# Zero stores sized by (batch, kv-heads), with four extra calls of 1.6 MB each: before the first softmax, after the output product of the last two groups and in the last group's K scores

## Chip, cores and metric

One Trainium2 chip, one core. The metric is device time of one execution in microseconds (us), lower is better. Runs are compared with runs of the kernel before on the same chip.

## The reference, cut to what matters

Decode attention over a window of the last W = 1024 of Sk = 4096 positions, in parallel with a GELU-gated MLP, forward and backward. Only the last 1024 positions of the K and V caches take part, so the gradients of the first 3072 are zero and have to be written:

```python
B, Sq, D = 4, 1, 512
Hq, Hkv, Sk, Dh = 32, 8, 4096, 128
W = min(4096, max(256, Sk // 4))                 # 1024
k = jnp.repeat(k_cache[:, :, Sk - W:, :], rep, axis=1)
v = jnp.repeat(v_cache[:, :, Sk - W:, :], rep, axis=1)
...
return x + _A_ref(xn, ...) + _B_ref(xn, ...)     # and jax.vjp of all of it
```

The gradients of K and V (out_2, out_3) are bfloat16 of 4 x 8 x 4096 x 128 each; their zero parts are 2 x 4 x 8 x 3072 x 128 x 2 B = 50.3 MB.

## The kernel before

The attention runs in NT = 4 groups t of two kv-heads. Loads go out on the sync engine, computed gradients on GpSimd, zeros on the scalar engine. Names in the profile: kb and vb are loads of K and V, osb_o and osb_q are staging tiles with gradients of the output and query weights, dx_b is the gradient of the input and the last thing computed, ztile holds the zeros. odq(t, 0) is the output product of group t with V (the recorded texts call the place after it the first "next-group product"), odq(t, 1) the dQ product. A zero store is placed behind the last scalar copy (`last`) that the program has at this point. The program text is no schedule: the build may move instructions of the compute engines within their engine.

```python
K0 = Sk - W                                   # 3072
outp = ctx.enter_context(tc.tile_pool(name="outp", bufs=3))   # staging of weight gradients (osb_o, osb_q, ...)
...
ZP = P // 2
ZW = K0 // ZP * Dh                            # 64 partitions of 12,288 B for one (batch, head)
...
ZG = 4
zlist = [(og, b, g) for b in range(B) for g in range(0, G, ZG) for og in (out_2, out_3)]   # 16 stores of 3.1 MB

def zeros(n):
    zs = ztile[0:P:P // ZP, :]
    zsrc = bass.AP(tensor=zs.tensor, offset=zs.offset, ap=[list(zs.ap[0]), [0, ZG], [1, ZW]])
    for _ in range(min(n, len(zlist))):
        og, b, g = zlist.pop(0)
        z = store(nc.scalar, og[b, g:g + ZG, 0:K0, :].rearrange("g (m j) d -> m g (j d)", m=ZP), zsrc, "zeros",
                  ["rest", "zeros"])
        tc.add_manual_dep(z.ins, last[-1].ins.name, ...)
...
def scores(t, k):                             # k = 0: K scores, k = 1: V (dP)
    for g in range(GP):
        for b in range(B):
            ...                               # transposes, copy, matmuls
            tick(2)                           # two pieces of deferred gradient work
            if b == 1 and (g, k) != (0, 0):
                zeros(1)
...
for t in range(NT):
    masks(t)
    scores(t, 0); softmax(t);   dvdk(t, 0)
    scores(t, 1); softmax_d(t); dvdk(t, 1)
    odq(t, 0)
    if t + 1 < NT: pre(t + 1)
    odq(t, 1); fin(t)
    load_next(t)                              # K, V of group t+1 (second head), K, V and weights of t+2
    dw(t)
tick(len(bg))
zeros(len(zlist))                             # whatever is left: 3 stores
```

Of the kernel before, what the change touches and what calls it, by code (L numbers as in the profile page):

```python
# [18 lines left out]
def kernel(  # L19
# [24 lines left out]
    nc = tc.nc  # L44

    B, Sq, D = A_x.shape
    _, G, Sk, Dh = A_k_cache.shape
# [4 lines left out]
    K0 = Sk - W  # L52
# [4 lines left out]
    GP = 2  # L57
    NT = G // GP
# [25 lines left out]
    def evac(out, in_, n, half=False, eng=None):  # L84

        eng = "dve" if half else eng
        ca, cd = (190 + n) / 1.2, (120 + (n / 2 if half else n)) / 0.96
        if eng is None:
            eng = "act" if load["act"] + ca <= load["dve"] + cd else "dve"
        load[eng] += ca if eng == "act" else cd  # L90
        if eng == "act":
            last.append(nc.scalar.copy(out=out, in_=in_))  # L92
            return last[-1]
        return nc.vector.tensor_copy(out=out, in_=in_)  # L94

    def store(eng, out, in_, kind, apart):

        d = eng.dma_start(out=out, in_=in_)  # L98
        for k in apart:
            tc.declare_no_dep(d.ins, group=k, reason="stores write disjoint parts of the outputs")  # L100
        tc.add_to_no_dep_group(kind, d.ins)
        return d
# [9 lines left out]
    for eng, dst, src in ((nc.sync, dy_b, grad_out), (nc.scalar, x_b, A_x)):  # L112
        eng.dma_start(out=dst[:], in_=bass.AP(tensor=src.tensor, offset=src.offset,
                                                  ap=[[D, B], [0, RB], [1, D]]))
# [42 lines left out]
    ZP = P // 2  # L157
    ZW = K0 // ZP * Dh
# [82 lines left out]
    def load_next(t):  # L241

        if t + 1 < NT:
            load_kv(t + 1, 0, 1)
            load_kv(t + 1, 1, 1)
        if t + 2 < NT:
            load_w(t + 2)
            load_kv(t + 2, 0, 0)
            load_kv(t + 2, 1, 0)


    ZG = 4
    zlist = [(og, b, g) for b in range(B) for g in range(0, G, ZG) for og in (out_2, out_3)]

    def zeros(n):

        zs = ztile[0:P:P // ZP, :]
        zsrc = bass.AP(tensor=zs.tensor, offset=zs.offset, ap=[list(zs.ap[0]), [0, ZG], [1, ZW]])
        for _ in range(min(n, len(zlist))):
            og, b, g = zlist.pop(0)  # L260
            z = store(nc.scalar, og[b, g:g + ZG, 0:K0, :].rearrange("g (m j) d -> m g (j d)", m=ZP), zsrc, "zeros",
                      ["rest", "zeros"])
            tc.add_manual_dep(z.ins, last[-1].ins.name,
                              mybir.DependencyInfo(mybir.DependencyClass.NoSync, mybir.DependencyReason.DATA))


    bg = deque()

    def tick(n):
        for _ in range(min(n, len(bg))):  # L270
            bg.popleft()()
# [51 lines left out]
    def scores(t, k):  # L323

        lf = (qm_all, dom_all)[k][t % 2][:].rearrange("p s c -> p (s c)")
        blks = (k_t, v_t)[k]
        ps = ps_a.tile([P, WQ], FP32, name="S_ps", tag=("S", "dP")[k])
        for g in range(GP):
            for b in range(B):
                T_ps = ps_w.tile([P, J, P], BF16, name="T_ps", tag="w")  # L330
                for j in range(J):
                    nc.tensor.transpose(T_ps[:, j, :], blks[(t, g)][:, b, j, :], ident[:])  # L332
                T_sb = tsb.tile([P, J * P], BF16, name="T_sb", tag="T", bufs=4)
                evac(T_sb[:], T_ps[:].rearrange("p j m -> p (j m)"), 1024, half=True)
                s = b * GP + g
                for q in range(NQ):
                    nc.tensor.matmul(ps[q * RG:(q + 1) * RG, :], lhsT=lf[:, s * RG:(s + 1) * RG],  # L337
                                     rhs=T_sb[:, q * WQ:(q + 1) * WQ], start=(g == 0 and b == 0),
                                     stop=(g == GP - 1 and b == B - 1), tile_position=(0, q * RG))
                tick(2)  # L340
                if b == 1 and (g, k) != (0, 0):
                    zeros(1)
        st[t][("S", "dP")[k]] = ps[:]

    def by_quarter(src, nm):
# [279 lines left out]
    for f4 in range(NF4):  # L625
        held = {}
        n = min(4, NF - 4 * f4)
# [5 lines left out]
    for srcT, wsb, og, nm in ((dhgT_b, wg_sb, out_6, "dhg_r"), (dhuT_b, wu_sb, out_7, "dhu_r")):  # L633
        s_r = f_rows(srcT, nm)
        for c in range(ND):
            held = {}
            for i in range(4):
                bg.append(lambda s_r=s_r, og=og, c=c, i=i, held=held: piece_g(s_r, og, c, i, held))
        for f2 in range(NF // 2):
            wT_ps = ps_w.tile([P, 2, ND, P], BF16, name="wgT_ps", tag="w")  # L640
            for i in range(2):
                fc = 2 * f2 + i
                for c in range(ND):
                    nc.tensor.transpose(wT_ps[:, i, c, :], wsb[:, c, fc * P:(fc + 1) * P], ident[:])  # L644
            wgT = tsb.tile([P, 2, ND, P], BF16, name="wgT", tag="wT")
            evac(wgT[:], wT_ps[:], 1024, half=True)
            for i in range(2):
                for c in range(ND):
                    nc.tensor.matmul(df_ps[:, c, :], lhsT=wgT[:, i, c, :], rhs=srcT[:, 2 * f2 + i, :],
                                     start=False, stop=False)  # L650
            tick(1)
            if f2 == NF // 2 - 1:
                zeros(1 if og is out_7 else 0)
    nc.tensor.matmul(df_ps[:].rearrange("p c b -> p (c b)"), start=False, stop=True, **edge)
    acc_add(1, df_ps[:])

# [1 line left out]
    with tc.tile_pool(name="stage", bufs=4, reuse_waits="tile") as stage, \  # L658
            tc.tile_pool(name="wodd", bufs=1, reuse_waits="tile") as wodd:
        wpool.append(wodd)  # L660
        load_w(1)
        for t in range(NT):
            if t == 0:
                pre(t)
            masks(t)
            scores(t, 0)
            softmax(t)
            dvdk(t, 0)
            scores(t, 1)
            softmax_d(t)  # L670
            dvdk(t, 1)
            odq(t, 0)
            if t + 1 < NT:
                pre(t + 1)
            odq(t, 1)
            fin(t)
            load_next(t)
            dw(t)
        tick(len(bg))
        zeros(len(zlist))  # L680


        acc_r = kvp.tile([P, 2, ND, B, RB], FP32, name="acc_r", tag="kb")
        nc.vector.tensor_copy(out=acc_r[:], in_=acc[:].unsqueeze(4).broadcast_to([P, 2, ND, B, RB]))
        fin_ps = []
        for o in range(2):
            f_ps = ps_w.tile([P, ND, P], FP32, name="f_ps", tag="w")
            for c in range(ND):
                nc.tensor.transpose(f_ps[:, c, :], acc_r[:, o, c].rearrange("p b r -> p (b r)"), ident_f[:])
            fin_ps.append(f_ps[:].rearrange("p c d -> p (c d)"))  # L690
        acc_o, acc_d = fin_ps
        out_b = kvp.tile([P, D], BF16, name="out_b", tag="vb")
        nc.vector.tensor_tensor(out=out_b[:], in0=acc_o, in1=x_b[:], op=ALU.add)
        nc.sync.dma_start(out=out_0.rearrange("b s d -> (b s) d"), in_=out_b[0:P:RB, :])

        s1 = const.tile([P, 1], FP32, name="s1")
        nc.vector.reduce_sum(out=s1[:], in_=acc_d, axis=AX.X)
        pr = kvp.tile([P, D], FP32, name="pr", tag="vb")
        s2 = const.tile([P, 1], FP32, name="s2")
        nc.vector.tensor_tensor_reduce(out=pr[:], in0=acc_d, in1=xn_f[:], scale=1.0, scalar=0.0,  # L700
                                       op0=ALU.mult, op1=ALU.add, accum_out=s2[:])
        nm1 = const.tile([P, 1], FP32, name="nm1")
        nc.vector.tensor_scalar(out=nm1[:], in0=s1[:], scalar1=-1.0 / D, scalar2=None, op0=ALU.mult)
        nm2 = const.tile([P, 1], FP32, name="nm2")
        nc.vector.tensor_scalar(out=nm2[:], in0=s2[:], scalar1=-1.0 / D, scalar2=None, op0=ALU.mult)
        nc.vector.scalar_tensor_tensor(out=pr[:], in0=xn_f[:], scalar=nm2[:, 0:1], in1=acc_d,
                                       op0=ALU.mult, op1=ALU.add)
        nc.vector.tensor_scalar(out=pr[:], in0=pr[:], scalar1=nm1[:, 0:1], scalar2=rstd[:, 0:1],
                                op0=ALU.add, op1=ALU.mult)
        dx_b = kvp.tile([P, D], BF16, name="dx_b", tag="kb")  # L710
        nc.vector.tensor_tensor(out=dx_b[:], in0=pr[:], in1=dy_b[:], op=ALU.add)
        nc.sync.dma_start(out=out_1.rearrange("b s d -> (b s) d"), in_=dx_b[0:P:RB, :])
# [30 lines left out]
```

## Time and profile before

| | before |
|---|---|
| time, median of 4 runs | 301.80 us (299.52 to 302.14) |
| span of the profiled run | 299.2 us |
| bytes moved, DMA busy (sum of the queues) | 112.38 MB, 96.3% = 288.1 us |
| end of the last compute step (store of dx_b issued) | 277.2 us |
| zero stores, of which issued at the end of the program (from 271.7 us) | 16, 3 |

The prediction shows the lines. The row DMA in the page's slices is the busy share of the core's 16 DMA engines in tenths; a 9 is full.

### The profile page before, as it was taken

The numbers are of one execution on the slowest core, as the hardware profiler recorded it, in microseconds if no ns is written. First come the engines' busy times: TensorE is split into PE (matmuls) and PEld (weight loads), VectorE is DVE, ScalarE is ACT, GpSimd is POOL, SyncE is SP. The second block draws the span as 40 slices with busy tenths as digits, with TensorE's granted clock in tenths as the row PEclk, the third lists the DMA queues.
The fourth block names the chain that finished last, engine by engine and source line by source line (L and its number), as shares of the span: only waits on it lengthen the run. The fifth ranks groups of instructions, "written<-read, shape, count | busy, mean of one in ns | idle before, by whom it ended". The sixth has DMA issues, their size and how long they took to land.

```text
span 299.2 us, 6821 instructions
## 1 busy us (share of the span) xinstructions
PE 208.5 (70%) x2956; PEld 142.3 (48%) x2956; DVE 145.5 (49%) x310; ACT 114.2 (38%) x217; POOL 66.7 (22%) x84
## 2 busy tenths in 40 slices
PE   1398995957969995838799873669995977981000
PEld 0386873625546763524576452337663645531000
DVE  5473671542563674325267731355674453786000
ACT  1202644533425464224156630434473541681000
POOL 6000121612130522300315230021513203141000
PEclk9985999885998799768699978597998796897555
DMA  5999999997999999999999999995979999699997
GB/s 144 383 384 381 386 401 426 401 425 312 369 418 350 358 387 423 415 424 424 416 379 347 398 432 418 424 431 209 350 274 396 404 402 408 238 344 377 416 429 320
DMA packets 30053, 112.38 MB, mean 376 GB/s; under 512 B 1408, under 2 KB 7560, under 8 KB 25928
## 3 DMA queue, kind: packets, MB, share of 16 engines
q10 hardware_dynamic: 4484, 50.46, 40.4%
q1 hardware_dynamic: 17732, 30.81, 28.7%
q0 software_dynamic: 7808, 30.67, 26.7%
q8 instruction: 23, 0.38, 0.5%
q14 instruction: 6, 0.05, 0.0%
HBM read 30.93 MB, written 81.01 MB: 374 GB/s over the span
## 4 chain that ended last, share of the span: by engine, by line
PE 50%; DMA 22%; DVE 12%; issue 4%; ACT 4%; POOL 1%; SPq 0%; DVEq 0%; ACTq 0%; POOLq 0%
DMA out_dram<-osb_o 14%; PE T_ps L332 10%; PE kv_ps L440 9%; PE S_ps L337 4%; DMA wd_sb<-in_B_w_down_dram 3%; PE od_ps L412 3%; PE wqT_ps L504 3%; DVE T_sb L94 3%; DMA out_dram<-osb_d 3%; PE acc_ps L181 3%; PE woT_ps L284 3%; PE wgT_ps L644 2%; PE wdT_ps L532 2%; DMA out_dram<-osb_g 2%; ACT stg_dk L92 1%
## 5 line engine op out<-in xcount | busy, mean ns | idle before, releaser
L94 DVE COPY T_sb<-T_ps 128x1024 bf16<-128x1024 bf16 x64 | 44.2, 691 | 33.3 <-PE T_ps L332 32.9
L92 ACT CAST stg_dv<-kv_ps 128x512 bf16<-128x512 f32 x52 | 28.9, 587 | 42.5 <-PE kv_ps L440 42.0
L332 PE MATMUL T_ps<-ident,vb 128*128 128x128 bf16 x256 | 27.1, 257 | 6.4 <-DVE osb_q L94 6.4
L92 ACT CAST stg_dk<-kv_ps 128x512 bf16<-128x512 f32 x46 | 25.0, 588 | 13.9 <-PE kv_ps L440 13.7
L332 PEld LDWEIGHTS <-vb 128*128 128x128 bf16 x256 | 20.9, 117 | 12.9 <-issue 9.4
L92 ACT CAST osb_q<-dwq_ps 128x512 bf16<-128x512 f32 x25 | 13.6, 589 | 29.6 <-DMA out_dram<-osb_o 19.5
L440 PE MATMUL kv_ps<-domr,P_q 128*128 128x512 bf16 x64 | 24.8, 452 | 0.0
L332 PE MATMUL T_ps<-ident,kb 128*128 128x128 bf16 x256 | 24.0, 223 | 0.6 <-ACT osb_g L92 0.3
L332 PEld LDWEIGHTS <-kb 128*128 128x128 bf16 x256 | 17.9, 99 | 12.6 <-issue 4.5
L92 ACT CAST osb_g<-dwg_ps 128x384 bf16<-128x384 f32 (+1 forms) x30 | 14.4, 536 | 16.6 <-PE dwg_ps L617 7.2
L440 PE MATMUL kv_ps<-qmr,dS_q 128*128 128x512 bf16 x64 | 19.9, 394 | 0.5 <-ACT stg_dv L92 0.2
L94 DVE COPY woT<-woT_ps 128x1024 bf16<-128x1024 bf16 x16 | 11.1, 692 | 16.3 <-PE woT_ps L284 16.3
L474 PE MATMUL dwq_ps<-od_r,xnm 128*128 128x256 bf16 x64 | 12.7, 322 | 6.3 <-DVE osb_q L94 6.2
L348 POOL TENSOR_TENSOR dS_q<-dS_b,qmsk 128x1024 bf16<-128x1024 bf16 x4 | 7.5, 1884 | 35.4 <-DVE dS_b L401 35.4
L92 ACT CAST osb_o<-dwo_ps 128x512 bf16<-128x512 f32 x23 | 12.9, 587 | 4.9 <-PE dwo_ps L459 4.4
L337 PE MATMUL S_ps<-T_sb,dom 128*32 128x256 bf16 x128 | 10.6, 316 | 4.4 <-DVE T_sb L94 4.3
L98 POOL DMA_DIRECT2D out_dram<-osb_q x8 | 5.9, 731 | 33.8 <-ACT osb_q L92 33.8
L94 DVE COPY wqT<-wqT_ps 128x1024 bf16<-128x1024 bf16 x16 | 11.0, 688 | 4.8 <-PE wqT_ps L504 4.5
L284 PE MATMUL woT_ps<-ident,wo_sb 128*128 128x128 bf16 x128 | 12.7, 247 | 0.9 <-ACT osb_g L92 0.6
L94 DVE CAST osb_q<-dwq_ps 128x512 bf16<-128x512 f32 x7 | 4.7, 689 | 16.7 <-DMA out_dram<-osb_o 16.5
L98 POOL DMA_DIRECT2D out_dram<-stg_dv x8 | 6.2, 774 | 29.2 <-ACT stg_dv L92 23.5
L94 DVE CAST stg_dk<-kv_ps 128x512 bf16<-128x512 f32 x18 | 12.1, 685 | 1.1 <-PE kv_ps L440 1.0
(187 smaller groups left out, 380.4 us busy)
## 6 DMA issues: line engine op xcount, KB each, us to landing
out_dram<-ztile ACTq DMA_DIRECT2D x16, 3072.0 KB, 17.0
kb<-in_A_k_cache_dram SPq DMA_DIRECT2D x8, 1024.0 KB, 13.1
vb<-in_A_v_cache_dram SPq DMA_DIRECT2D x8, 1024.0 KB, 13.9
out_dram<-stg_dv POOLq DMA_DIRECT2D x8, 1024.0 KB, 7.3
out_dram<-stg_dk POOLq DMA_DIRECT2D x8, 1024.0 KB, 7.9
wo_sb<-in_A_wo_dram SPq DMA_DIRECT2D x4, 1024.0 KB, 14.0
wq_sb<-in_A_wq_dram SPq DMA_DIRECT2D x4, 1024.0 KB, 15.1
out_dram<-osb_o POOLq DMA_DIRECT2D x8, 512.0 KB, 14.6
```

Of the source, the lines that this page charges most:

```text
L92: last.append(nc.scalar.copy(out=out, in_=in_))
L94: return nc.vector.tensor_copy(out=out, in_=in_)
L98: d = eng.dma_start(out=out, in_=in_)
L181: nc.tensor.matmul(ps[:, c, :], lhsT=lf(c), rhs=rhs, start=(k == 0), stop=(k == len(terms) - 1))
L284: nc.tensor.transpose(wT_ps[:, i, c, :], wo_sb[:, 2 * h2 + i, c * P:(c + 1) * P], ident[:])
L332: nc.tensor.transpose(T_ps[:, j, :], blks[(t, g)][:, b, j, :], ident[:])
L337: nc.tensor.matmul(ps[q * RG:(q + 1) * RG, :], lhsT=lf[:, s * RG:(s + 1) * RG], rhs=T_sb[:, q * WQ:(q + 1) * WQ], start=(g == 0 and b == 0 ...
L348: nc.gpsimd.tensor_tensor(out=dst[:], in0=src[:].unsqueeze(1).broadcast_to([P, NQ, WQ]), in1=qmsk[:].unsqueeze(2).broadcast_to([P, NQ, WQ] ...
L412: nc.tensor.matmul(od_ps[b * RB:b * RB + rep, k, g, :], lhsT=pT[:, jj, c0:c0 + rep], rhs=blks[(t, g)][:, b, j, :], start=(j == 0), stop=(j ...
L440: nc.tensor.matmul(mps[:].rearrange("p b d -> p (b d)"), lhsT=src[:, q, jj * P:(jj + 1) * P], rhs=mr[:, g].rearrange("p b d -> p (b d)"), ...
L474: nc.tensor.matmul(mps[:, i].rearrange("p g d -> p (g d)"), lhsT=xnm[:, i2 * 2 + i, c * P:(c + 1) * P], rhs=dq_r[:].rearrange("p g d -> p ...
L504: nc.tensor.transpose(wT_ps[:, i, c, :], wq_sb[:, c, h * Dh:(h + 1) * Dh], ident[:])
```

## The change

The intent: zeros are work without inputs, so they can be issued at any time. The change counts them in units of one (batch, kv-head), 0.786 MB, lets a call ask for 2 units as well as 4, and adds four calls of 2 units at places where the DMA engines would run dry.

```diff
-    ZG = 4
-    zlist = [(og, b, g) for b in range(B) for g in range(0, G, ZG) for og in (out_2, out_3)]
+    zruns = deque([og, b, 0] for b in range(B) for og in (out_2, out_3))
     def zeros(n):
         zs = ztile[0:P:P // ZP, :]
-        zsrc = bass.AP(..., ap=[list(zs.ap[0]), [0, ZG], [1, ZW]])
-        for _ in range(min(n, len(zlist))):
-            og, b, g = zlist.pop(0)
-            z = store(nc.scalar, og[b, g:g + ZG, 0:K0, :]...)
+        while n > 0 and zruns:
+            og, b, g = zruns[0]
+            w = min(n, G - g, GP * 2)
+            zsrc = bass.AP(..., ap=[list(zs.ap[0]), [0, w], [1, ZW]])
+            z = store(nc.scalar, og[b, g:g + w, 0:K0, :]...)
             tc.add_manual_dep(...)
+            n -= w
+            zruns[0][2] += w
+            if zruns[0][2] == G:
+                zruns.popleft()
@@ scores
-                if b == 1 and (g, k) != (0, 0):
-                    zeros(1)
+                if b == 1:
+                    zeros(4 if (g, k) != (0, 0) else 2 if t == NT - 1 else 0)
@@ end of the MLP
-                zeros(1 if og is out_7 else 0)
+                zeros(4 if og is out_7 else 0)
@@ main loop
             scores(t, 0)
+            zeros(2 if t == 0 else 0)
             softmax(t)
...
             odq(t, 0)
+            zeros(2 if t >= NT - 2 else 0)
             if t + 1 < NT:
                 pre(t + 1)
@@ end
-        zeros(len(zlist))
+        zeros(2 * B * G)
```

More of the change, by code (lines that the diff above doesn't have):

```diff
@@ L249, in load_next @@
             load_kv(t + 2, 1, 0)
-    ZG = 4
-    zlist = [(og, b, g) for b in range(B) for g in range(0, G, ZG) for og in (out_2, out_3)]
+    zruns = deque([og, b, 0] for b in range(B) for og in (out_2, out_3))
     def zeros(n):
         zs = ztile[0:P:P // ZP, :]
-        zsrc = bass.AP(tensor=zs.tensor, offset=zs.offset, ap=[list(zs.ap[0]), [0, ZG], [1, ZW]])
-        for _ in range(min(n, len(zlist))):
-            og, b, g = zlist.pop(0)
-            z = store(nc.scalar, og[b, g:g + ZG, 0:K0, :].rearrange("g (m j) d -> m g (j d)", m=ZP), zsrc, "zeros",
+        while n > 0 and zruns:
+            og, b, g = zruns[0]
+            w = min(n, G - g, GP * 2)
+            zsrc = bass.AP(tensor=zs.tensor, offset=zs.offset, ap=[list(zs.ap[0]), [0, w], [1, ZW]])
+            z = store(nc.scalar, og[b, g:g + w, 0:K0, :].rearrange("g (m j) d -> m g (j d)", m=ZP), zsrc, "zeros",
                       ["rest", "zeros"])
```

## The prediction

> **What bounds the kernel now.** I read the page first, by its slices and its queues. The rows are the busy tenths of TensorE, the busy tenths of the 16 DMA engines, and their rate, in 40 slices of 7.48 us; then what each DMA queue moved.
>
> ```profile
> PE   1398995957969995838799873669995977981000
> ...
> DMA  5999999997999999999999999995979999699997
> GB/s 144 383 384 381 386 401 426 401 425 312 369 418 350 358 387 423 415 424 424 416 379 347 398 432 418 424 431 209 350 274 396 404 402 408 238 344 377 416 429 320
> ...
> q10 hardware_dynamic: 4484, 50.46, 40.4%
> q1 hardware_dynamic: 17732, 30.81, 28.7%
> q0 software_dynamic: 7808, 30.67, 26.7%
> ```
>
> The three queues keep the DMA engines busy for 95.8% of the span, so this is a kernel bound by how many bytes it moves (112.38 MB in 299.2 us). Nearly half of them are zeros: q10 is the scalar engine's queue, and it carries the zero stores (16 of 3.146 MB, 50.3 MB), while q1 has the loads of the sync engine and q0 the computed gradients. The last three digits of PE are 0: the last 20 us have no compute at all. What they hold is in the timeline of ACT and in the waits of SP:
>
> ```profile
> 271.71 0.61 ACTq L98 DMA_DIRECT2D out_dram<-ztile  x1
> ...
> 272.36 2.63 ACTq L98 DMA_DIRECT2D out_dram<-ztile  x2
> ```
>
> ```profile
> SPq L738 <- DMA out_dram<-ztile: 13.7, 2, 7.3
> ```
>
> Three of the 16 zero stores, 9.4 MB, are issued when the compute is over, and the kernel ends by waiting for them. So the end of the span is a drain of zeros; the compute ends at 277.2 us (the last line of the chain below plus its length).
>
> But the DMA engines were not always busy before. The view by stretches, with the DMA share in the column before the last, finds the holes of the third row above (columns: stretch, length, busy time of the five engines, PE clock, DMA share, GB/s):
>
> ```profile
> 72.00:76.00 4.00, 4.00 (x31) 2.39 (x30) 1.72 (x3) 1.99 (x5) 0.86 (x2) 0.56 0.35 145
> ...
> 204.00:208.00 4.00, 3.96 (x88) 2.96 (x86) 1.98 (x3) 2.25 (x5) 0.00 (x0) 0.85 0.55 219
> 208.00:212.00 4.00, 3.26 (x106) 2.62 (x103) 1.75 (x7) 0.77 (x3) 3.14 (x3) 1.00 0.67 199
> ...
> 220.00:224.00 4.00, 3.99 (x48) 2.36 (x45) 3.08 (x5) 2.52 (x5) 0.75 (x1) 1.00 0.41 162
> ...
> 256.00:260.00 4.00, 3.81 (x53) 2.38 (x51) 2.99 (x6) 2.34 (x6) 0.75 (x1) 0.95 0.37 141
> 260.00:264.00 4.00, 3.60 (x14) 1.17 (x13) 3.90 (x7) 3.86 (x9) 0.75 (x1) 1.00 0.83 312
> ...
> 272.00:296.00 24.00, 1.09 (x8) 0.86 (x8) 5.04 (x11) 0.74 (x2) 0.72 (x1) 0.53 1.02 419
> ```
>
> In the holes TensorE is busy and DMA has nothing to do; in the drain it is the reverse, at 419 GB/s. Lost DMA time is length times (1 - share): 2.6 us at 72; 1.8 + 1.3 = 3.1 us at 204 to 212; 2.4 us at 220; 2.5 + 0.7 = 3.2 us at 256 to 264. **Sum 11.3 us.** All stretches between these have shares of 0.96 to 1.06.
>
> Last, the chain of waits in order of time, to see where the compute itself waits for DMA:
>
> ```profile
> 113.26 17.74 DMA out_dram<-osb_o
> ...
> 169.62 18.59 DMA out_dram<-osb_o
> ...
> 267.10 4.47 DMA out_dram<-osb_o
> ...
> 276.48 0.69 DVE dx_b L711
> ```
>
> Between 76 and 190 us the compute waits twice for an output store to free one of three staging buffers, and DMA is full there. From 190 to 267 the chain has no DMA piece: compute leads and DMA has slack.
>
> **What the Trainium skill says.** (1) "DMA: Bandwidth & Descriptors", section "Issuing engines are not separate DMA queues": transfers of all issuing engines run on the same 16 DMA engines and interleave. The trace agrees: the three queues' shares add up to one. (2) Same page, "Queues, rings and completion order": each engine round-robins over its queues at packet granularity. By the queue lines a zero packet is 50.46 MB / 4484 = 11.3 KB, a gradient packet 3.9 KB, a load packet 1.7 KB; where all three run (172 to 192 us) the trace's records give about 290, 93 and 50 GB/s, nearly these proportions. So zeros take two thirds while they are in flight; that is why a 0.5 MB store takes 16 to 20 us to land there. (3) Same page, "Why a DMA increments its semaphore by 16 and not by 1": the number of engines used follows from the slowest dimension of the access pattern. That stays 64 partitions in the new stores (the heads are a later dimension), so smaller ones still use all 16 engines; the trace of before shows full share with such a pattern alone (0.98 to 1.02 after 280 us).
>
> **The change, part by part.** A unit is one (batch, head): 3072 x 128 x 2 B = 0.786 MB; there are 64. Before, each call stores 4 units; 13 calls fall inside the compute, 3 at the end. I walked through the new code by hand.
> - *The old 13 calls* still store 4 units each at the same places. As the requests no longer line up with runs of 8 heads, six of them split in two stores of 2 units. The total is 24 issues instead of 16. An issue is 0.61 us on the scalar queue, 8 x 0.61 = 4.9 us spread over a span in which ACT is 38% busy: off the path. Bytes and packets are the same.
> - *The new calls* are four of 2 units (1.57 MB, or 1.57/0.419 = 3.75 us of DMA at the drain's rate): before the first softmax, after the first next-group product of the last two groups, and in the last K scores. Together 6.29 MB, 15.0 us.
> - *The end* then has 4 units left, 3.15 MB, instead of 12.
>
> A zero store is placed behind the last scalar copy that precedes it in the program. By the timeline of ACT that means issue near 65.5, 198, 217 and 244 us, all into a queue that is about to run dry: in front of each of the four holes. What each fills, carrying over the excess:
> - 72 to 76: 3.75 us offered, 2.6 us of hole; 1.1 us goes on top of a stretch that is already full, so compute and everything after it slips by up to 1.1 us, without a loss to the DMA total.
> - 204 to 212: 3.75 offered, 3.1 filled, 0.6 carried.
> - 220 to 224: 3.75 + 0.6 offered, 2.4 filled, 1.9 carried.
> - 256 to 264: 3.75 + 1.9 offered, 3.2 filled, 2.4 carried into the last gradient stores.
>
> So all four holes can be filled, and of the 15.0 us taken from the drain 11.3 us are gained; the other 3.7 us are the same work done earlier in a full queue. The last wait for an osb_o store (4.47 us) grows by the 2.4 us carried and the slip, so compute ends near 281 instead of 277 us. The final 3.15 MB are issued then, with gradient stores still in flight, so DMA doesn't run dry; the end is still the zero drain, now about 7 us long.
> Sum: 301.77 - 11.3 = 290.5 us if nothing leaks. I take off a little for gaps at queue changes (the shares of 0.96 to 0.98 beside the holes): **290.9 us**, -3.6%.
>
> **Rivals.**
> - *A: the zeros crowd the loads and stores that compute needs.* For: the 18 us waits for osb_o stand exactly where zeros are in flight, and the last group's K and V loads (issued 208.6 to 210.2) meet new zeros. Against: the 198 us store is ahead of those loads and drains by about 208; the K load takes some 7 us while its second half is only needed near 222; from 190 on the chain has slack against DMA. If the compute of the last group slipped by 4 us, it would still end inside the time that DMA needs anyway. Should two such waits appear and reopen holes, half the gain is lost: 296 us.
> - *B: loads wait for zero stores through shared semaphores.* The compiled program of the kernel before gives the DMAs of the sync and scalar engines eight completion semaphores in turn, so each waits until the eighth before it has landed; one such wait shows:
>
> ```profile
> SPq L237 <- DMA out_dram<-ztile: 13.9, 1, 13.9
> ```
>
> It is hidden there, since the same load then waits 31.0 us for TensorE. Eight more zero stores shift this rotation. Counting the new order by hand, every load finds its eighth predecessor landed 15 us or more before; so I expect nothing. If I miscounted one: some 3 to 8 us, 294 to 298 us.
> - *C: the drain stays, because the compute is the bound.* If the last stores all came out of compute late, the end would be compute plus receipts: 277.2 + 2 + about 9 us for the last zeros. That is 288, not more than the DMA count gives, so it changes little. It would only bind if the slip reached 4 us or more.
> - *D: more than computed.* Zeros mixed with gradient stores move at 410 to 430 GB/s against 312 to 366 for the gradients alone at 260 to 272 us; some of the carried work could cost less than counted: 288 us.
>
> **Range and chances.** The DMA count is a balance of bytes and does not depend on details; a leak comes from a hole that is only half filled (one is 2.4 to 3.2 us) or a new wait. One hole lost and some noise give 294.5; D gives 288. Range 287.5 to 295.0. Faster by over 2% (under 295.7) 0.92, within 2% 0.07, slower 0.01.
>
> **What would show it.** DMA share near 1 at 72 to 76 and from 200 to 272; 24 zero stores of which one, of 3 MB, follows the compute; the drain without compute 6 to 10 us instead of 20; compute ending 2 to 6 us later than 277; the osb_o waits near 113 and 170 about as long as before. I am wrong if holes reappear at other times, if SP shows waits for ztile in front of loads, or if the total of DMA busy time grows.

## The result, and the profile after

The changed kernel takes **289.57 us** (median of 4 runs, 288.33 to 291.58) against 301.80 us. The ratio is 0.9617, 95% interval 0.9544 to 0.9689. Ratios here are the mean time of one kernel's fast runs over that of the other's fast runs of the same rounds, so not quite the ratio of the medians. A repeat with more rounds (below) gave 0.9655. The profiled run was the fastest of its four: its span is 286.6 us, those of the others 287.8 to 289.9.

The page of the changed kernel: slices of TensorE and DMA, and its zero stores (count, size, microseconds from issue to landing).

```profile
PE   1297995985978998637699987576998686599620
...
DMA  5999999999999999999999999999999999998996
...
out_dram<-ztile ACTq DMA_DIRECT2D x8, 3072.0 KB, 16.5
out_dram<-ztile ACTq DMA_DIRECT2D x16, 1536.0 KB, 14.3
```

The 7, the 5, the second 7 and the 6 inside the row DMA are gone; what is left is an 8 near 260 us. The empty slices at the end of PE are one instead of three. There are 24 zero stores, as counted.

The view by stretches of the changed kernel (stretch, length, busy time of PE, PEld, DVE, ACT and POOL, PE clock, DMA share, GB/s):

```profile
72.00:76.00 4.00, 4.00 (x41) 2.83 (x37) 2.08 (x3) 1.87 (x4) 0.58 (x1) 0.72 1.05 439
...
204.00:208.00 4.00, 3.35 (x92) 2.11 (x91) 1.89 (x3) 1.94 (x4) 0.00 (x0) 1.00 0.99 378
...
220.00:224.00 4.00, 2.72 (x34) 1.75 (x33) 1.98 (x3) 1.82 (x4) 0.75 (x1) 1.00 1.01 425
...
260.00:264.00 4.00, 3.77 (x37) 1.73 (x38) 3.38 (x6) 3.01 (x6) 0.89 (x2) 1.00 0.72 275
264.00:272.00 8.00, 5.85 (x29) 2.58 (x27) 5.92 (x10) 5.63 (x11) 3.62 (x5) 1.00 0.93 348
272.00:283.00 11.00, 1.97 (x8) 1.57 (x8) 5.45 (x11) 1.07 (x2) 0.72 (x1) 0.51 1.01 401
```

The holes at 72, 204 to 212 and 220 are full. That at 256 to 264 has moved to 260 to 272, and 4 x 0.28 + 8 x 0.07 = 1.7 us of it are left. The timeline shows the last zero store, now alone, and the last store of the compute:

```profile
273.78 0.61 ACTq L98 DMA_DIRECT2D out_dram<-ztile  x1
...
279.98 0.52 SPq L719 DMA_DIRECT2D out_dram<-dx_b  x1
```

Compute ends 2.8 us later than before (277.2), the span 12.6 us earlier. The last zero store is issued 6.2 us before the compute ends. The three of before (271.7 to 273.6 us) also went out ahead of that end, though the prediction calls them issued "when the compute is over".

The end has also changed its kind. Before, the sync engine waited for zeros last (13.7 us, in the prediction); now it waits for a gradient store:

```profile
SPq L745 <- DMA out_dram<-osb_q: 4.6, 1, 4.6
```

By the semaphore events of the traces, the last zeros landed at 298.2 us before, 13.9 us behind the last gradient store. Now the last zeros land at 284.8, dx_b at 285.2 and the last weight gradient at 285.3 us: zeros and computed stores end together.

The pieces of the chain of waits that are a wait for osb_o:

```profile
112.24 18.02 DMA out_dram<-osb_o
...
168.68 18.20 DMA out_dram<-osb_o
...
224.14 14.32 DMA out_dram<-osb_o
...
268.82 4.81 DMA out_dram<-osb_o
```

The first two and the last are as before within half a microsecond; the one at 224 us is new.

Where the 12.6 us of the two profiled runs come from: the sum of the queues' busy shares was 96.3% of 299.2 us (288.1 us) and is 42.1 + 29.7 + 27.2 + 0.5 = 99.5% of 286.6 us (285.2 us). By this count, time in which DMA was not busy fell from 11.1 to 1.4 us, which is 9.7 us, and the same bytes took 2.9 us less. Only the differences mean something: the share in the long full stretches is 1.02 to 1.04, and the first 4 us alone have 0.15 before and 0.13 after, which is 3.4 and 3.5 us idle.

One thing came with the change that its text does not show: comparing the two compiled instruction lists, TensorE's order differs in the third and fourth group (the build put the dQ products of the third group before the transposes of the next weights, and a few weight-gradient products behind K transposes). The K and V loads of the last group are issued at 204.6 us instead of 208.6. This is a second change; an experiment below takes out its part in the third group.

### The profile page after: what moved, and what is told of

It reads as the page before. It is cut to its first block, busy times and chain, and to the rows that moved or that the text cites. A ratio compares the mean times of both kernels' runs of the same rounds, so it can differ in the third digit from the quotient of the medians.

```text
span 286.6 us, 6818 instructions
## 1 busy us (share of the span) xinstructions
PE 208.1 (73%) x2946; PEld 142.4 (50%) x2956; DVE 145.1 (51%) x310; ACT 113.8 (40%) x217; POOL 66.7 (23%) x84
## 2 busy tenths in 40 slices
DMA packets 30181, 112.38 MB, mean 392 GB/s; under 512 B 1536, under 2 KB 7688, under 8 KB 26056
## 3 DMA queue, kind: packets, MB, share of 16 engines
q10 hardware_dynamic: 4612, 50.46, 42.1%
q1 hardware_dynamic: 17732, 30.81, 29.7%
q0 software_dynamic: 7808, 30.67, 27.2%
## 4 chain that ended last, share of the span: by engine, by line
PE 47%; DMA 28%; DVE 13%; issue 5%; ACT 3%; POOL 1%; SPq 0%; DVEq 0%; ACTq 0%; POOLq 0%
DMA out_dram<-osb_o 19%; PE T_ps L337 8%; PE kv_ps L445 8%; DVE T_sb L94 4%; DMA wd_sb<-in_B_w_down_dram 4%; PE S_ps L342 4%; PE wqT_ps L509 3%; PE od_ps L417 3%; DMA out_dram<-osb_d 3%; PE acc_ps L181 3%; PE woT_ps L289 3%; PE wgT_ps L649 2%; PE wdT_ps L537 2%; DMA out_dram<-osb_g 2%; ACT stg_dk L92 2%
## 5 line engine op out<-in xcount | busy, mean ns | idle before, releaser
L92 ACT CAST osb_g<-dwg_ps 128x384 bf16<-128x384 f32 (+1 forms) x30 | 14.5, 534 | 16.6 <-PE dwg_ps L622 6.8
L94 DVE COPY woT<-woT_ps 128x1024 bf16<-128x1024 bf16 x16 | 11.1, 692 | 18.4 <-PE woT_ps L289 18.4
L479 PE MATMUL dwq_ps<-od_r,xnm 128*128 128x256 bf16 x64 | 13.4, 338 | 8.8 <-DVE osb_q L94 8.7
L445 PE MATMUL kv_ps<-qmr,dS_q 128*128 128x512 bf16 x59 | 18.9, 395 | 0.9 <-ACT stg_dv L92 0.3
L342 PE MATMUL S_ps<-T_sb,dom 128*32 128x256 bf16 x128 | 10.5, 313 | 4.4 <-DVE T_sb L94 4.4
L509 PEld LDWEIGHTS <-wq_sb 128*128 128x128 bf16 x128 | 10.4, 115 | 4.7 <-issue 3.5
## 6 DMA issues: line engine op xcount, KB each, us to landing
out_dram<-ztile ACTq DMA_DIRECT2D x16, 1536.0 KB, 14.3
kb<-in_A_k_cache_dram SPq DMA_DIRECT2D x8, 1024.0 KB, 13.9
```

What stands on the lines that cost most here:

```text
L92: last.append(nc.scalar.copy(out=out, in_=in_))
L94: return nc.vector.tensor_copy(out=out, in_=in_)
L342: nc.tensor.matmul(ps[q * RG:(q + 1) * RG, :], lhsT=lf[:, s * RG:(s + 1) * RG], rhs=T_sb[:, q * WQ:(q + 1) * WQ], start=(g == 0 and b == 0 ...
L445: nc.tensor.matmul(mps[:].rearrange("p b d -> p (b d)"), lhsT=src[:, q, jj * P:(jj + 1) * P], rhs=mr[:, g].rearrange("p b d -> p (b d)"), ...
L479: nc.tensor.matmul(mps[:, i].rearrange("p g d -> p (g d)"), lhsT=xnm[:, i2 * 2 + i, c * P:(c + 1) * P], rhs=dq_r[:].rearrange("p g d -> p ...
L509: nc.tensor.transpose(wT_ps[:, i, c, :], wq_sb[:, c, h * Dh:(h + 1) * Dh], ident[:])
```

## The experiments

Theory: before, DMA work was missing in four holes while a drain of zeros without compute stood at the end; each extra call fills the hole behind it. Rivals: it is the new order of the stores; it is their size; it is the shorter drain wherever the zeros go; it is the changed instruction order.

### Order alone, and size alone

```diff
 # order_only: new zeros(), old places
-zeros(4 if (g, k) != (0, 0) else 2 if t == NT - 1 else 0)
+zeros(4 if (g, k) != (0, 0) else 0)
-zeros(2 if t == 0 else 0)
-zeros(2 if t >= NT - 2 else 0)
 # halves: the same and
-w = min(n, G - g, GP * 2)
+w = min(n, G - g, GP)
```

> Only the new order of the zero stores (all heads of one batch and output in a row, instead of alternating between the two outputs); no new calls, all 16 stores of 3 MB where they were, three of them at the end; the instruction order of TensorE, VectorE and GpSimd is that of before. Theory (the gain comes from filling the holes in the DMA time): same as before, ratio 0.997 to 1.003, holes at 72, 204 to 212, 220 and 256 to 264 us as before. Rival (the new order of addresses lets the memory take the zeros faster): ratio below 0.99 and zeros above 430 GB/s in the drain.

> The kernel of before in places and bytes (new order of the stores, no new calls), but each store of 4 units cut into two of 2 units: 32 zero stores of 1.5 MB. TensorE's order is that of before. Theory (size does not matter, they queue back to back over all 16 engines): ratio 0.997 to 1.004; 16 more issues of 0.61 us on the scalar queue stay hidden. Rival (smaller stores let the other queues in sooner, or cost a fixed time each): the osb_o waits near 112 and 169 us change by more than 2 us, or the ratio leaves 0.99 to 1.01.

Measured: order_only 299.98 us, ratio 1.0031 (0.9976 to 1.0086); halves 299.30 us, ratio 0.9978 (0.9927 to 1.0028). In both the instruction order of TensorE is that of before. In halves the osb_o waits are 17.4 and 17.6 us, against 17.7 and 18.6. Neither the order nor the size of the zero stores moves the time by more than the noise of half a per cent.

### The same zeros, in a place that is full

```diff
-zeros(4 if (g, k) != (0, 0) else 2 if t == NT - 1 else 0)
+zeros((6 if t == 1 else 4) if (g, k) != (0, 0) else 0)
-zeros(2 if t == 0 else 0)
-zeros(2 if t >= NT - 2 else 0)
+zeros(2 if t == 1 else 0)
```

> The control: the same 8 extra units (6.3 MB) leave the drain, but all go to the second group (112 to 160 us), where the DMA engines are already full: 6 units instead of 4 in its three calls and 2 after its first next-group product. Theory (only holes give time): the compute behind is pushed back by about the 15 us that the zeros take, the holes after 200 us stay, merely later, and the gain is small: the hole at 72 us remains too, ratio 0.98 to 1.00 (296 to 302 us). Rival (what counts is that the drain gets shorter, whatever the place): as the changed kernel, ratio 0.96 (290 us).

Measured: 299.63 us, ratio 1.0001 (0.9949 to 1.0052). The drain is as short as in the changed kernel (one store left, issued at 285.1 us), and nothing is gained. Its stretches show why, same columns as above:

```profile
72.00:76.00 4.00, 4.00 (x36) 2.57 (x32) 1.66 (x3) 1.89 (x4) 0.58 (x1) 0.60 0.48 199
...
216.00:224.00 8.00, 7.22 (x167) 5.25 (x166) 3.92 (x9) 3.40 (x7) 1.81 (x2) 0.84 0.63 206
232.00:240.00 8.00, 7.42 (x81) 4.20 (x80) 5.59 (x9) 5.42 (x10) 1.50 (x2) 1.00 0.76 295
268.00:280.00 12.00, 11.17 (x82) 5.39 (x81) 10.18 (x17) 9.47 (x18) 2.26 (x3) 0.93 0.71 271
```

All four holes are still there, the later ones pushed back by about 12 us: 2.1 + 3.0 + 1.9 + 3.5 = 10.5 us, where before had 11.3. The compute behind the extra zeros slipped by nearly what the drain lost (dx_b issued at 290.6 us, 13.4 later). (In this trace TensorE's order differs from before by a few instructions of the second group.) So shortening the drain is worth nothing by itself; the place decides.

### Each extra call alone

Each kernel keeps one of the four calls and has the others at 0.

> Only the extra call of 2 units before the first softmax. Theory: it fills the hole at 72 to 76 us, 2.6 us, and the rest of its 3.75 us pushes the later work: ratio 0.991 (299.1 us), range 0.987 to 0.995. Rival (zeros in the full middle crowd the loads and stores and are paid back): ratio 1.00. Rival (the drain's length counts): 3.75 us, ratio 0.9875.

> Only the extra call after the first product of the third group (the scheduler also moves that group's dQ products ahead of the next group's transposes, as in the changed kernel). Theory: it fills the 3.1 us of hole at 204 to 212 us, ratio 0.990 (298.7 us), range 0.986 to 0.994, with the hole at 220 still there. Rival (the earlier K and V loads that the new instruction order brings are what helps, not the zeros): more than 3.75 us, compute ending earlier than 277 us by 2 us or more.

> Only the extra call of 2 units in the last group's K scores, near 217 us. Theory: it fills the 2.4 us hole at 220 to 224 and carries 1.3 us into the hole at 256 to 264: up to 3.7 us, ratio 0.988 to 0.992 (say 0.990). Rival (zeros that now run while the gradient stores of the third group leave make the compute wait for a staging buffer, as the new 14.3 us osb_o piece in the changed kernel's chain): the chain shows an osb_o piece near 224 us and compute ends 1 to 2 us later; if that wait costs time, ratio 0.995 or more.

> Only the extra call after the last group's first product, near 244 us; the instruction order of the compute engines is that of before. Theory: fills the 3.2 us hole at 256 to 264, ratio 0.989 (range 0.986 to 0.993), hole at 220 unchanged. Rival (the last gradient stores are held up by it and the final wait for osb_o grows by as much): the compute end moves from 277 to 279 or later and the ratio is above 0.994.

| call kept | time, us | ratio (95%) | off 300 us | hole predicted |
|---|---|---|---|---|
| soft_only | 296.13 | 0.9891 (0.9842 to 0.9941) | 3.3 | 2.6 |
| odq2_only | 297.10 | 0.9927 (0.9881 to 0.9974) | 2.2 | 3.1 |
| kscore3_only | 297.85 | 0.9932 (0.9889 to 0.9975) | 2.0 | 2.4, up to 3.7 |
| odq3_only | 296.70 | 0.9895 (0.9858 to 0.9931) | 3.2 | 3.2 |

The intervals are 1.1 to 1.5 us to either side, so single rows are no closer than that. kscore3_only lies just outside its expected 0.988 to 0.992. The product of the four ratios is 0.965, by the four intervals to about 0.009 either way; the changed kernel had 0.9617 and 0.9655. They add up within that.

The stretches show that each call fills its own hole and leaves the others. First soft_only, which fills 72 but not 204:

```profile
72.00:76.00 4.00, 4.00 (x41) 2.83 (x37) 2.01 (x3) 1.86 (x4) 0.58 (x1) 0.70 1.01 422
204.00:212.00 8.00, 7.22 (x184) 5.38 (x183) 4.46 (x12) 3.63 (x8) 4.34 (x3) 0.99 0.66 226
```

Then odq2_only, which fills 204 to 212, but its next hole is now 8 x 0.45 = 3.6 us wide instead of 2.4, so a part was given back:

```profile
204.00:212.00 8.00, 7.64 (x159) 5.45 (x160) 3.85 (x10) 2.56 (x6) 1.51 (x2) 0.71 1.00 342
216.00:224.00 8.00, 7.99 (x111) 5.25 (x111) 5.80 (x10) 4.70 (x10) 1.55 (x2) 1.00 0.55 208
```

Then kscore3_only:

```profile
220.00:224.00 4.00, 2.67 (x29) 1.68 (x29) 2.14 (x4) 1.97 (x4) 0.75 (x1) 1.00 1.00 419
```

And odq3_only. Its compute did end 2 us later (dx_b at 279.1 us), as its rival had it, but the time that the rival added to that did not come (0.9895, not above 0.994):

```profile
256.00:264.00 8.00, 7.37 (x68) 4.13 (x68) 6.19 (x12) 6.13 (x12) 1.50 (x2) 0.92 0.99 390
```

The rival in the expectation of kscore3_only fell: its chain has no osb_o piece near 224 us, while odq2_only has one of 11.5 us. (By the traces, kscore3_only has the changed TensorE order of the fourth group, and no run separates that from its zeros.) The side rival of odq2_only, that the earlier loads are what helps, is not supported either: its gain is below 3.75 us and its compute did not end earlier (its last osb_o wait starts at 268.1 us, that of before at 267.1).

### The changed kernel again, and with TensorE's order of before

```diff
 # kept_order: the third group's 2 units join the call before them
-zeros(4 if (g, k) != (0, 0) else 2 if t == NT - 1 else 0)
+zeros((6 if (t, g, k) == (NT - 2, 1, 1) else 4) if (g, k) != (0, 0) else 2 if t == NT - 1 else 0)
-zeros(2 if t >= NT - 2 else 0)
+zeros(2 if t == NT - 1 else 0)
```

> The changed kernel once more, unaltered, with more rounds and on the chip of the next three runs. It is there to have its ratio beside theirs: 0.958 to 0.966. In its first look a wait of 14.3 us for an osb_o store stands in the chain at 224 us that the prediction did not have; it should be there again if it is a property of the kernel.

> The changed kernel with the 2 units of the third group's call issued some 3 us earlier, as 6 units instead of 4 in the call before it. Through this TensorE, in the third group, keeps the instruction order of before (the changed kernel has the dQ products ahead of the transposes of the next group's weights there); the bytes in each hole stay the same. Theory (the holes make the gain): ratio within 0.005 of the changed kernel's in the same call. Rival (the reordering, which releases the K and V buffers 4 us earlier, makes part of the gain): 0.967 or more. Side question: if the osb_o wait at 224 us comes from the reordering, it is gone here; if it comes from the zeros, it stays.

Measured: after_again 289.73 us, 0.9655 (0.9604 to 0.9706); kept_order 289.06 us, 0.9623 (0.9577 to 0.9669). (One of the six runs of after_again, 294.12 us, is counted as slow.) They are the same within the noise. So no part of the gain is seen to come from the changed order in the third group. The profile of kept_order, of one of its slower runs (span 288.0 us), has a share of 0.74 from 256 to 272 us, 4.2 us empty where the changed kernel has 1.8; so "the bytes in each hole stay the same" did not hold for this one. In after_again the wait for osb_o at 224 us is there again, 14.4 us. The chain of kept_order has the new wait as well:

```profile
222.32 15.49 DMA out_dram<-osb_o
```

The reordering of the third group therefore does not cause it. Neither does the K-score call alone (kscore3_only has none). Of the kernels with three buffers, it was in each that has the third group's 2 extra units before the last group, and in no other, so it comes with those zeros. (In the fourth group kept_order still has the changed order; what that is worth was not tested.)

### One unit more into the rest of the last hole

```diff
             load_next(t)
+            zeros(1 if t == NT - 1 else 0)
             dw(t)
```

> The changed kernel with one of its last four units (0.79 MB, 1.9 us of DMA) issued earlier, after the last group's weight products, so that it lies in what is left of the hole at 260 to 272 us. Theory: it fills up to 1.6 us of it, against a later landing of the last osb_o store by as much, which moves the compute's end but not the drain's: ratio 0.953 to 0.960. Rival (the last stores are on the path now): compute ends later and the drain's end stays, ratio 0.961 to 0.965.

Measured: 289.39 us, ratio 0.9643 (0.9614 to 0.9672): no gain, and none of the expected 1.6 us. The ratio lies in the range of the rival (0.961 to 0.965). The unit was issued at 261.4 us, but 2.6 us were idle from 260 to 272, against 1.7:

```profile
260.00:272.00 12.00, 9.28 (x72) 4.28 (x72) 9.95 (x17) 8.57 (x16) 2.26 (x3) 0.99 0.78 302
```

Compute came later, as the rival had it: the last wait for osb_o starts at 272.3 us instead of 268.8, and dx_b is issued at 283.0. The zeros are in at 285.8 us, the last gradient at 286.6 and dx_b at 286.8: the zeros no longer come last. The granted clock of TensorE was 0.50 from 256 to 260 in that run. Whether the clock or the zeros held compute up was not separated.

### A fourth staging buffer, with the change and without

```diff
-outp = ctx.enter_context(tc.tile_pool(name="outp", bufs=3))
+outp = ctx.enter_context(tc.tile_pool(name="outp", bufs=4))
```

> The changed kernel with four staging buffers for the weight-gradient stores instead of three; TensorE's order is that of the changed kernel. It takes away the waits for osb_o in the chain (near 112, 169, 224 and 269 us). Theory (DMA is full between 72 and 260, so these waits cost nothing there): compute ends earlier by some us, but the total moves by less than the remaining holes allow, 0 to 2 us: ratio to before 0.955 to 0.962, beside 0.9617 of the changed kernel. Rival (the waits for osb_o are what remains of the critical path): ratio below 0.945, 5 us or more gained.

> The kernel of before with four staging buffers for the weight gradients instead of three. With the changed kernel this took the osb_o waits away, and three waits for K loads of 23 to 48 us took their place, and it became slower. Theory now (the osb_o wait paces the zero stores: without it compute issues the next ones sooner, and they crowd the K loads): the chain here shows kb pieces too and no osb_o, and the ratio is 0.995 to 1.015, no gain. Rival (the K waits come only from the extra zeros of the change): no kb pieces, compute ends earlier, ratio 0.98 to 0.995.

Measured: bufs4 (with the change) 294.89 us median, ratio 0.9707 (0.9655 to 0.9759), which rests on only two of its six runs, 290.48 and 292.08; the other four (294.9 to 296.3 us) lie over 1.5% above the fastest and are counted as slow. before_bufs4 293.56 us median, ratio 0.9749 (0.9696 to 0.9802), four of six runs fast. Both profiles fell in runs counted as slow, though the clock of these runs is no lower. They are read here for the kind of their waits; what they show explains these runs and is not shown for the fast ones.

Both of my expectations on the time were wrong. With the change the fourth buffer gains nothing, where I had expected 0.955 to 0.962; whether it costs time is not settled by two fast runs, as the interval overlaps those of after_again (to 0.9706) and tail_one (to 0.9672). Without the change it gains 2.5%, where I had put no gain (the verdict is unclear only because the interval crosses the 2% mark). The part on the waits was right: the osb_o waits are gone and waits for K loads stand in their place. The chain of bufs4:

```profile
101.73 47.63 DMA kb<-in_A_k_cache_dram
...
163.35 40.26 DMA kb<-in_A_k_cache_dram
203.68 23.39 DMA kb<-in_A_k_cache_dram
```

and that of before_bufs4, two pieces of less than half the total:

```profile
132.09 26.12 DMA kb<-in_A_k_cache_dram
195.33 19.38 DMA kb<-in_A_k_cache_dram
```

In bufs4 the last zero stores from the V scores of the second and third group are issued at 126.2 and near 185 us (after: 137.0 and 192.2), and the chain no longer has a stop for a buffer. The loads take longer to land: the longest V load took 55.9 us (45.0 after, 20.6 before), and the next V load, which needs the completion semaphore of that one, waited for it. The waits of the sync engine and the stretch that follows in bufs4:

```profile
SPq L237 <- DMA vb<-in_A_v_cache_dram: 16.6, 1, 16.6
```

```profile
220.00:236.00 16.00, 7.23 (x57) 4.02 (x57) 4.31 (x7) 3.23 (x6) 0.75 (x1) 0.63 0.49 184
```

In this slow run a new hole of 16 x 0.51 = 8.2 us opened: compute waits for its loads, and while it waits no zeros are issued, as they are tied to its progress. In before_bufs4, again in a slow run, the hole at 72 us is gone (share 1.03) and compute ends at 270.4 us instead of 277.2, but a hole of 6.0 us stands at 208 to 220.

What follows: the waits for osb_o are not free, as I had taken them to be; a fourth buffer alone is worth 2.5%, the change 3.5 to 3.8%. But the two do not add (0.9707 together). That the extra zeros then delay the loads is argued from one slow run. A version with four buffers and other places for the zeros was not run; whether it beats 289 us stays open.

## Why the prediction was right, point by point

- **The bound and the sum.** 11.3 us of holes, 290.9 us predicted, 289.57 us measured. The gain was 12.2 us by the first medians, and 10.3 us by the repeat (0.9655 of 299.4 us). That holes are what the extra zeros fill is shown by full_place (same bytes out of the drain, ratio 1.0001) and by the four single calls (product 0.965).
- **The sizes of the terms.** Of the four holes, three were filled wholly. In the last I had 3.2 us filled and 2.4 us carried on; in fact 1.7 us stayed empty. Taken with the smaller leaks (shares of 0.96 to 0.99), 9.3 us came from the holes by the view of stretches (9.7 by the queues' sums). The rest, 3 us in the profiled pair and about 1 us by the repeat, is another thing: the same bytes took 2.9 us less DMA time. So the sum came out close partly by luck: the holes gave some 2 us less than counted, and a term that was not counted made up for it. By queue (share times span) the gradients went from 79.9 to 78.0 us, the loads from 85.9 to 85.1, the zeros from 120.9 to 120.7. after_again repeats it with 284.7 us in all, while order_only and halves have 287.4 and 287.3. That it happened is shown; its cause is open. Rival D named zeros mixed with the last gradient stores, and the runs speak against that: odq3_only, which has just this, took 97.6% of 296.9 = 289.8 us, and before_bufs4, without any extra zeros, 96.5% of 294.7 = 284.4 us (a slow run).
- **The end of the compute.** Predicted near 281 us, found at 279.98, but for another reason. I expected the last osb_o wait to grow by 2.4 us; it went from 4.47 to 4.81. Instead the wait of 14.3 us at 224 us appeared, after a statement that the chain has no DMA piece between 190 and 267 us. This is rival A in a mild form: compute ended 2.8 us later in all, which the DMA count absorbed.
- **Rival B, shared semaphores.** I wrote that every load's eighth predecessor lands 15 us or more before. For the last K load that held: its predecessor landed 18.4 us before the load was free to go. For the last V load it did not: by the semaphore events its predecessor, the V load issued at 159.4 us, took 41.6 us and landed 4.0 us before the issue at 205.0 us; another load, of weights at 158.4 us, had its predecessor (45.0 us) landed 4.2 us before. I had used the landing times of the kernel before, but the added zeros lengthen them. It cost nothing here; in bufs4 it was a wait of 16.6 us, for a V load that took 55.9 us.
- **Rival C** came to a tie, and that the end "is still the zero drain" was wrong: zeros, dx_b and the last weight gradient land within 0.6 us of each other. The rival's sum gave the last store 2 us to land, a figure that no run here shows; dx_b took 5.2 us (279.98 to 285.16). So C comes level already at a slip of 2.8 us and not of 4, and tail_one, which took more from the drain, gained nothing.
- **Smaller readings.** For 172 to 192 us the trace gives 291, 92 and 43 GB/s, not 50 for the loads; the split is near the packet sizes there, but from 113 to 131 us it is 238, 100 and 84. At 92 GB/s a 0.5 MB store alone would take 5.7 us (an estimate from these numbers), so the 18 us waits are not explained by the split alone; older gradient stores were still in flight (1 MB from 110.7 to 125.4 us, when the osb_o store was issued at 113.3). And the packets are not quite the same: 30,181 instead of 30,053, 16 for each of the 8 stores more.
- **What I left unsaid was wrong:** that waits for staging buffers in a full stretch cost nothing. before_bufs4 at 0.9749 says otherwise. In its profile (a slow run) the hole at 72 us is closed and compute ends 6.8 us earlier; that this is what gains the time in the fast runs is not shown.

## What to carry to other kernels

When a kernel that is bound by transfers ends in a drain of work without inputs, find the stretches where the DMA engines idle while compute is busy, and issue that work just ahead of them; the idle time, not the length of the drain, is what can be gained. Test it with the same bytes moved into a full stretch. Look at what lands last: once computed results and bulk land together, as here within 0.6 us, moving more of the bulk forward can gain nothing, as in tail_one. And treat a buffer wait as a possible pacer of bulk stores: taking it away may let the bulk run ahead of the loads that compute needs next, as in the profile of bufs4.

## What the Trainium skill lacked or had wrong

- "DMA: Bandwidth & Descriptors" says that queues of several engines interleave and that spreading over them only saves issue time. It does not draw the consequence of arbitration by packet: a queue of large packets can take most of the rate. Here, from 172 to 192 us, zeros in packets of 11.3 KB on average (rows of 12,288 B) got 291 of 427 GB/s beside gradients (3.9 KB, 92) and loads (1.7 KB, 43), with 490, 492 and 436 packets begun. From 113 to 131 us it was 238, 100 and 84 GB/s, so the proportion does not hold everywhere. In the changed kernel a 1 MB load took up to 45.0 us to land, 55.9 us with four buffers (a slow run), against 20.6 us for the slowest V load before.
- The same page describes a packet as preferably 4096 B or less (section "SWDGE vs HWDGE vs iDMA", for the GpSimd path). For trn2 it gives no size in bytes for the queues of the sync and scalar engines; the profile counts records of 12,288 B on the scalar engine's. Whether such a record is a packet as the page means it is not shown.
- The same page asks for transfers of 1 MiB or more. It does not say whether more helps when DMAs queue back to back. We saw no effect above that size: stores of 1.6 MB instead of 3.1 MB, ratio 0.9978.
- No page has it that loads and stores of the sync and scalar engines can share a small set of completion semaphores in turn (eight in these programs), so that a load can wait for an unrelated earlier transfer: 13.9 us in the kernel before (hidden), 16.6 us in bufs4 (not hidden; a slow run).
